# Attention block on one core: keys laid on the partitions for the scores, where queries lay before

## The chip, the cores and the metric

The kernel runs on one core of a Trainium2 chip. Its engines each run their own stream of instructions and meet through semaphores: TensorE (PE, matmuls and weight loads), VectorE (DVE), ScalarE (ACT), GpSimd (POOL) and SyncE (SP, which here issues DMAs). The metric is device time in microseconds (us) of one launch; lower is better.

## What is computed

The reference, cut to what matters (bfloat16 inputs; B = 8 batches of 112 queries, 32 heads of 192, 512 cached keys, model width 640):

```python
q = (x @ wq).reshape(8, 112, 32, 192).transpose(0, 2, 1, 3)
scores = einsum("bhqd,bhkd->bhqk", q, k_cache) * 192 ** -0.5
p = softmax(scores)                          # over the 512 keys
o = einsum("bhqk,bhkd->bhqd", p, v_cache)
out = o.transpose(0, 2, 1, 3).reshape(8, 112, 32 * 192) @ wo
```

The caches hold 50 MB each, wq and wo 7.9 MB each.

## The kernel before

`build_mha_kernel` works on pairs of heads: 4 groups of 8 heads, in each group 8 batches, in each batch 4 pairs, 128 pairs in all. Every engine's program is a loop over pairs (`run_program`), in which each stage has a fixed place and a lag: `DEFAULT_ORDERS` lists for each engine which stage of which pair is issued in one period. The order is written out by hand, and each stage begins with waits on semaphores (`W`).

For one pair the stages are:

- **Q** (`pe_Q`, L262): 15 matmuls of 112 columns give q transposed (head dimension on the partitions) for two heads; ACT copies it out (L272) and DVE makes four half copies (L323 to L326), so that each head of 192 stands as one chunk of 128 and one half-filled chunk.
- **S** (`pe_S`, L166 to L169): 8 matmuls of 256 columns with q as weights and K as moving operand. Scores come with the 112 queries on the partitions and 512 keys along the row. K has been transposed on its way in by the DMA (`issue_k`, L477).
- **Softmax**: DVE finds each row's maximum while it copies the scores (L332), ACT takes the exponential and the row sum (L284), DVE the reciprocal (L344) and, per head, a diagonal matrix of reciprocals (L308).
- **PT** (`pe_PT`, L182): 8 matmuls with the probabilities as weights and the diagonal as moving operand transpose and normalise at once; ACT (L278) and DVE (L338) copy the result out.
- **PV** (`pe_PV`, L200 and L206): 16 matmuls of 112 columns with V as weights; L206 uses 64 columns of the array for each of two heads. ACT copies the output out (L291).
- **O** (`pe_O`, L234 and L235): 6 matmuls of 512 and 128 columns with wo, accumulated over the 4 pairs of a batch; after the last of them DVE adds the sum to `acc` in float32 (L373 to L377, `dve_oacc`), and in the last group writes the output tile.

K and V come in blocks of 4 heads (768 KB each) on SP's queue, into six buffers each; a block is issued when the block that used its buffer has been consumed. The weights come on POOL's queue, paced by waits on the K and V blocks. x is transposed by TensorE at the start (L402, L409).

Of the kernel before, what the change touches and what calls it, by code (L numbers as in the profile page):

```python
# [5 lines left out]

BF16 = mybir.dt.bfloat16
F32 = mybir.dt.float32
ACTF = mybir.ActivationFunctionType
ALU = mybir.AluOpType  # L10

DEFAULT_ORDERS = dict(
    PE=[("S", 0), ("PT0", -1), ("PV", -2), ("PT1", -1), ("O", -3), ("Q", 2)],
# [7 lines left out]
def build_mha_kernel(nc, x, k_cache, v_cache, wq, wo, out, cfg=None):  # L21
    cfg = dict(cfg or {})
    B, SQ, D = x.shape
    _, H, SK, DH = k_cache.shape
# [3 lines left out]
    DC = D // 128  # L28
# [8 lines left out]
    scale = float(DH) ** -0.5  # L37
# [31 lines left out]

    with ExitStack() as es:  # L70
        def sb(name, shape, dt):
            return es.enter_context(nc.sbuf_tensor(name, shape, dt))

        def sem(name):
            return es.enter_context(nc.semaphore(name))

        WQC = HG * DH
        wq_sb = sb("wq_sb", [128, 2, DC, WQC], BF16)
        wo_sb = sb("wo_sb", [128, 2, 3 * PPU, D], BF16)
        OUTT = cfg.get("OUTT", False)  # L80
        if OUTT:
            accT = sb("accT", [128, B, DC, SQ], F32)
            oTf = sb("oTf", [128, 2, DC, SQ], BF16)
            acc = None
        else:
            acc = sb("acc", [SQ, B, D], F32)
        xT_sb = sb("xT_sb", [128, DC, B * SQ], BF16)
        kt = [sb(f"kt{j}", [128, 2, 3, G * 128], BF16) for j in range(NKB)]
        vt = [sb(f"vt{j}", [128, G, 768], BF16) for j in range(NVB)]
        qs = sb("qs", [128, NQ, NSLOT, SQ], BF16)  # L90
        s_sb = sb("s_sb", [SQ, NSS, SK], F32)
        p_sb = sb("p_sb", [SQ, NP, SK], BF16)
# [4 lines left out]
        ident = sb("ident", [128, 128], BF16)  # L97
        nmx = sb("nmx", [SQ, NS], F32)
        rsum = sb("rsum", [SQ, NS], F32)
        rinv = sb("rinv", [SQ, NS], F32)  # L100
        ps = es.enter_context(nc.psum_tensor("ps", [128, 8, 512], F32))

        sS = sem("sS"); sPT = sem("sPT"); sPV = sem("sPV"); sO = sem("sO"); sQ = sem("sQ")
        dSM = sem("dSM"); dDG = sem("dDG"); dQC = sem("dQC"); dPTE = sem("dPTE"); dOA = sem("dOA"); dRC = sem("dRC")
        aEX = sem("aEX"); aQE = sem("aQE"); aPTE = sem("aPTE"); aPVE = sem("aPVE")
        gI0 = sem("gI0"); gINIT = sem("gINIT"); dINIT = sem("dINIT")
        sOF = sem("sOF"); aOF = sem("aOF")
        mX = sem("mX")
# [4 lines left out]
        mK = [sem(f"mK{j}") for j in range(NKB)]  # L113
        mV = [sem(f"mV{j}") for j in range(NVB)]
        mOUT = [sem(f"mOUT{j}") for j in range(2)]
# [3 lines left out]
        mWQ = [sem(f"mWQ{j}") for j in range(min(2, NHG) * PPU)]  # L119
        mWO = [sem(f"mWO{j}") for j in range(min(2, NHG) * PPU)]  # L120
# [23 lines left out]
        block = es.enter_context(nc.Block())  # L144

        def W(eng, s, v):
            if v > 0:
                eng.wait_ge(s, v)
# [120 lines left out]
        def act_evacQ(act, ip):  # L269
            W(act, sQ, ip + 1)  # L270
            W(act, sS, 2 * (ip - NQ) + 2)
            act.activation(qs[:, ip % NQ, 0:3, :], ps[:, 5, 0:3 * SQ].rearrange("p (c s) -> p c s", c=3),  # L272
                           ACTF.Copy).then_inc(aQE, 1)

        def act_evacpT0(act, ip):
            W(act, sPT, 2 * ip + 1)
            W(act, sPV, ip - NPT + 1)
            act.activation(pT_sb[:, ip % NPT, 0, :], ps[:, 2, 0:4 * SQ], ACTF.Copy).then_inc(aPTE, 1)  # L278

        def act_exp(act, i, h):  # L280
            Hh = 2 * i + h
            W(act, dSM, Hh + 1)
            W(act, sPT, Hh - NP + 1)
            act.activation(p_sb[:, Hh % NP, :], s_sb[:, Hh % NSS, :], ACTF.Exp,  # L284
                           bias=nmx[:, Hh % NS:Hh % NS + 1], scale=-1.0,
                           accum_out=rsum[:, Hh % NS:Hh % NS + 1]).then_inc(aEX, 1)

        def act_evacPV(act, ip):
            W(act, sPV, ip + 1)
            W(act, sO, ip - NO + 1)  # L290
            act.activation(oT_sb[:, ip % NO, :, :], ps[:, 4, 0:3 * SQ].rearrange("p (c s) -> p c s", c=3),  # L291
                           ACTF.Copy).then_inc(aPVE, 1)

        def act_evacOF(act, ip):
# [3 lines left out]
            W(act, sOF, b + 1)  # L298
            act.activation(o_out[:, b, :], psb[0:SQ, 7, 256:256 + D], ACTF.Copy).then_inc(aOF, 1)

# [3 lines left out]
        def dve_diag(dve, ip, h):  # L304
# [3 lines left out]
            dve.tensor_scalar(dg[:, Hh % ND, :], ident[0:SQ, 0:SQ], rinv[:, Hh % NS:Hh % NS + 1], None,  # L308
                              op0=ALU.mult).then_inc(dDG, 1)

# [17 lines left out]
        def dve_smax(dve, i, h):  # L328
            Hh = 2 * i + h
            W(dve, sS, Hh + 1)  # L330
            W(dve, aEX, Hh - NSS + 1)
            dve.tensor_scalar(s_sb[:, Hh % NSS, :], ps[0:SQ, h, :], -scale, None, op0=ALU.mult,  # L332
                              op1=ALU.min, accum_out=nmx[:, Hh % NS:Hh % NS + 1]).then_inc(dSM, 1)

# [11 lines left out]
        def dve_oacc(dve, ip):  # L346
# [6 lines left out]
            if OUTT:  # L353
# [3 lines left out]
                for k, (src, cs) in enumerate(parts):  # L357
# [6 lines left out]
                    else:  # L364
                        ins = dve.tensor_tensor(dst, src, accT[:, b, cs, :], op=ALU.add)
                ins.then_inc(dOA, 1)
                return
            parts = [(ps[0:SQ, 6, :], slice(0, 512)), (ps[0:SQ, 7, 0:128], slice(512, 640))]
            for k, (src, cs) in enumerate(parts):
# [4 lines left out]
                elif hg < NHG - 1:  # L374
                    ins = dve.tensor_tensor(acc[:, b, cs], src, acc[:, b, cs], op=ALU.add)
                else:
                    ins = dve.tensor_tensor(o_out[:, b, cs], src, acc[:, b, cs], op=ALU.add)  # L377
            ins.then_inc(dOA, 1)
# [5 lines left out]
        psb = ps[:].bitcast(BF16)  # L384
# [27 lines left out]
        def run_program(eng, stages, order, hook=None, post_hook=None):  # L412
            for i in PER:
                if hook is not None:
                    hook(eng, i)
                for st, lag in order:
                    ip = i + lag
                    if ok(ip):
                        stages[st](eng, ip)
                if post_hook is not None:  # L420
                    post_hook(eng, i)
# [24 lines left out]
        def _(act):  # L446
            W(act, dINIT, 1)
            act.activation(dummy[:, 2:3], dummy[:, 0:1], ACTF.Exp)
            run_program(act, ACT_STAGES, orders["ACT"])
# [211 lines left out]
    return nc  # L661


def bass_standalone__mha_block_cached__near_ridge_kernel(
    nc: bass.Bass,
    x: bass.AP,
    k_cache: bass.AP,
    v_cache: bass.AP,
    wq: bass.AP,
    wo: bass.AP,  # L670
    out: bass.AP,
):
    return build_mha_kernel(nc, x, k_cache, v_cache, wq, wo, out)


# [26 lines left out]
```

## Time and profile before

| What | Value |
|---|---|
| median of 3 runs | 500.41 us (499.59 to 500.98) |
| span of the profiled execution, first to last instruction | 499.2 us |
| TensorE busy, share of the span | 96% |
| VectorE, ScalarE, GpSimd | 89%, 71%, 14% |
| bytes moved by DMA, mean rate | 119.90 MB, 240 GB/s |
| mean granted TensorE clock | 0.999 |

The page of the profile counts each engine's busy time, cuts the span in 40 slices, follows the chain of work that ended last back from the last instruction, and groups instructions by line, engine and shape, with the mean duration of one and the idle time before it. The timeline lists instructions in order of time and merges neighbours of one line ("x8"). Matmuls are pipelined: one starts while the one before it is still passing through the array, so the cost of a matmul in a dense stretch is the distance between two starts, not its duration.

### The profile page before, as it was taken

The page shows a single profiled execution, that of the slowest core. Times are in us where ns is not written, and L with a number is a line of the kernel's source. Part 1 is how long each engine was busy: PE and PEld are TensorE (multiplying, and loading weights), DVE is VectorE, ACT ScalarE, POOL GpSimd, SP SyncE. Part 2 cuts the span into 40 slices and gives each one's busy share as a digit, 9 for nine tenths or more (in the row PEclk, how much of TensorE's full clock was granted, in tenths as well). Part 3 has the DMA queues.
Part 4 walks back from the last instruction along what each step waited for, and adds up shares of the span by engine and source line. Part 5 has one row for each costly group of instructions (what it writes and reads, how often), then busy time and mean ns, then how long its engine had stood idle before and what let it go on. Part 6 is the DMA issues. An engine that isn't in the chain of part 4 may idle for free.

```text
span 499.2 us, 18678 instructions
## 1 busy us (share of the span) xinstructions
PE 479.0 (96%) x6824; PEld 418.9 (84%) x6824; DVE 446.6 (89%) x1610; ACT 355.1 (71%) x898; POOL 71.5 (14%) x133
## 2 busy tenths in 40 slices
PE   1799999999999999999999999999999999999995
PEld 1788888888888888888888888888888888888884
DVE  2589999998999999999999999999999999999994
ACT  1277777777777777777777777777777777777773
POOL 7110133131000133131000122322000000000000
PEclk9999999999999999999999999999999999999999
DMA  9999999999999999999999999999999999999000
GB/s 227 305 285 239 244 256 274 249 265 292 237 249 263 281 261 259 245 265 251 239 247 236 259 290 279 240 282 260 233 272 254 255 260 255 238 258 261 3 14 25
DMA packets 239738, 119.90 MB, mean 240 GB/s; under 512 B 201840, under 2 KB 236480, under 8 KB 239648
## 3 DMA queue, kind: packets, MB, share of 16 engines
q1 hardware_dynamic: 233472, 101.82, 94.4%
q0 software_dynamic: 6176, 16.88, 11.3%
q8 instruction: 56, 0.92, 0.8%
q14 instruction: 34, 0.28, 0.2%
HBM read 67.21 MB, written 1.15 MB: 137 GB/s over the span
## 4 chain that ended last, share of the span: by engine, by line
PE 93%; DMA 2%; issue 1%; DVE 1%; POOL 1%; ACT 0%; DVEq 0%; POOLq 0%; ACTq 0%
PE ps L262 19%; PE ps L234 16%; PE ps L182 13%; PE ps L200 10%; PE ps L206 8%; PE ps L166 6%; PE ps L169 6%; PE ps L167 6%; PE ps L168 6%; PE ps L235 4%; DMA wq_sb<-in_wq_dram 2%; DVE xT_sb L409 1%; POOL wq_sb L578 0%; DVE s_sb L332 0%; DVE o_out L377 0%
## 5 line engine op out<-in xcount | busy, mean ns | idle before, releaser
L284 ACT ACTIVATE p_sb<-s_sb,nmx 112x512 bf16<-112x512 f32 x256 | 181.6, 712 | 3.1 <-DVE s_sb L332 2.1
L332 DVE TENSOR_SCALAR_CACHE_REDUCE s_sb<-ps 112x512 f32<-112x512 f32 x256 | 166.3, 686 | 16.2 <-PE ps L169 14.0
L278 ACT ACTIVATE pT_sb<-ps 128x448 bf16<-128x448 f32 x128 | 69.5, 543 | 88.4 <-PE ps L182 88.4
L262 PE MATMUL ps<-xT_sb,wq_sb 128*128 128x112 bf16 x1920 | 118.0, 215 | 5.2 <-DMA wq_sb<-in_wq_dram 5.2
L234 PE MATMUL ps<-wo_sb,oT_sb 128*112 128x512 bf16 x384 | 118.3, 380 | 0.0
L262 PEld LDWEIGHTS ps<-xT_sb,wq_sb 128*128 128x128 bf16 x1920 | 103.8, 99 | 16.7 <-DMA wq_sb<-in_wq_dram 4.4
L182 PE MATMUL ps<-dg,p_sb 112*128 112x112 bf16 x1024 | 94.0, 214 | 1.8 <-ACT p_sb L284 1.6
L272 ACT ACTIVATE qs<-ps 128x336 bf16<-128x336 f32 x128 | 57.6, 450 | 45.0 <-PE ps L262 41.8
L338 DVE CAST pT_sb<-ps 128x448 bf16<-128x448 f32 x128 | 79.9, 624 | 5.3 <-PE ps L182 1.4
L235 PE MATMUL ps<-wo_sb,oT_sb 128*112 128x128 bf16 x384 | 83.9, 219 | 0.0
L182 PEld LDWEIGHTS ps<-dg,p_sb 112*128 112x128 bf16 x1024 | 64.5, 98 | 14.4 <-ACT p_sb L284 1.9
L166 PE MATMUL ps<-kt,qs 128*112 128x256 bf16 x256 | 70.8, 277 | 2.5 <-issue 1.9
L200 PE MATMUL ps<-pT_sb,vt 128*128 128x112 bf16 x1024 | 71.8, 213 | 0.1
L167 PE MATMUL ps<-kt,qs 128*112 128x256 bf16 x256 | 70.4, 275 | 0.0
L169 PE MATMUL ps<-kt,qs 128*112 128x256 bf16 x256 | 70.4, 275 | 0.0
L168 PE MATMUL ps<-kt,qs 128*112 128x256 bf16 x256 | 70.3, 275 | 0.0
L234 PEld LDWEIGHTS ps<-wo_sb,oT_sb 128*112 128x112 bf16 x384 | 49.7, 129 | 22.3
L581 POOL DMA_DIRECT2D wq_sb<-in_wq_dram x60 | 32.1, 539 | 188.5 <-DMA kt<-in_k_cache_dram 182.4
L308 DVE TENSOR_SCALAR dg<-ident,rinv 112x112 bf16<-112x112 bf16 x256 | 52.9, 249 | 5.0 <-issue 0.5
L200 PEld LDWEIGHTS ps<-pT_sb,vt 128*128 128x128 bf16 x1024 | 56.5, 98 | 0.9 <-issue 0.5
L291 ACT ACTIVATE oT_sb<-ps 128x336 bf16<-128x336 f32 x128 | 55.3, 432 | 1.7 <-PE ps L206 1.7
L235 PEld LDWEIGHTS ps<-wo_sb,oT_sb 128*112 128x112 bf16 x384 | 50.0, 130 | 0.0
(38 smaller groups left out, 498.5 us busy)
## 6 DMA issues: line engine op xcount, KB each, us to landing
vt<-in_v_cache_dram SPq DMA_DIRECT2D x64, 768.0 KB, 5.8
wq_sb<-in_wq_dram POOLq DMA_DIRECT2D x60, 96.0 KB, 5.3
wo_sb<-in_wo_dram POOLq DMA_DIRECT2D x24, 160.0 KB, 5.6
wo_sb<-in_wo_dram POOLq DMA_DIRECT2D x32, 80.0 KB, 5.1
wq_sb<-in_wq_dram POOLq DMA_DIRECT2D x4, 480.0 KB, 10.2
wo_sb<-in_wo_dram POOLq DMA_DIRECT2D x4, 320.0 KB, 10.9
out_dram<-o_out SPq DMA_DIRECT2D x8, 140.0 KB, 4.4
kt<-in_k_cache_dram SPq DMA_TRANSPOSE x64, 9.9
```

Source lines behind the costliest of these rows:

```text
L166: pe.matmul(bk[:, 0:256], qs[:, qb, EA[h], :], ktb[:, :, 0, cs], start=True, stop=False)
L167: pe.matmul(bk[:, 0:256], qs[:, qb, ET[h], :], ktb[:, :, 1, cs], start=False, stop=True)
L168: pe.matmul(bk[:, 256:512], qs[:, qb, OC[h], :], ktb[:, :, 2, cs], start=True, stop=False)
L169: pe.matmul(bk[:, 256:512], qs[:, qb, OH[h], :], ktb[:, :, 1, cs], start=False, stop=True).then_inc(sS, 1)
L182: mm = pe.matmul(ps[:, 2 + h, j * SQ:(j + 1) * SQ], p_sb[:, pslot, j * 128:(j + 1) * 128], dg[:, dslot, :], start=True, stop=True)
L200: pe.matmul(ps[:, 4, oc * SQ:(oc + 1) * SQ], vtb[:, u, q * 192: q * 192 + 128], pT_sb[:, ptb, h, j * SQ:(j + 1) * SQ], start=(j == 0), sto ...
L234: pe.matmul(ps[0:SQ, 6, :], oT_sb[:, ob, c, :], wo_sb[:, wb, 3 * lp + c, 0:512], start=first, stop=last)
L235: mm = pe.matmul(ps[0:SQ, 7, 0:128], oT_sb[:, ob, c, :], wo_sb[:, wb, 3 * lp + c, 512:640], start=first, stop=last)
L262: mm = pe.matmul(ps[:, 5, c * SQ:(c + 1) * SQ], lhsT, xT_sb[:, dc, b * SQ:(b + 1) * SQ], start=(dc == 0), stop=(dc == DC - 1))
L284: act.activation(p_sb[:, Hh % NP, :], s_sb[:, Hh % NSS, :], ACTF.Exp, bias=nmx[:, Hh % NS:Hh % NS + 1], scale=-1.0, accum_out=rsum[:, Hh % ...
L332: dve.tensor_scalar(s_sb[:, Hh % NSS, :], ps[0:SQ, h, :], -scale, None, op0=ALU.mult, op1=ALU.min, accum_out=nmx[:, Hh % NS:Hh % NS + 1]). ...
L338: dve.tensor_copy(pT_sb[:, ip % NPT, 1, :], ps[:, 3, 0:4 * SQ]).then_inc(dPTE, 1)
```

## The change

A new function `build_main` computes the whole block; the old `build_mha_kernel` stays behind it as a second path. It runs only if a flag says that some sum of exponentials fell out of the range 2^-30 to 2^40.

```diff
-    return build_mha_kernel(nc, x, k_cache, v_cache, wq, wo, out)
+    with nc.sbuf_tensor("flag", [1, 1], I32) as flag:
+        build_main(nc, x, k_cache, v_cache, wq, wo, out, flag)
+        raised = nc.values_load(flag[0:1, 0:1], ...)
+        with nc.If(raised != 0):
+            build_mha_kernel(nc, x, k_cache, v_cache, wq, wo, out)
```

`build_main` works in 64 units: 8 groups of 4 heads, in each 8 batches. Head `a` of a unit has the band of partitions 32a to 32a+31.

- **K** comes in whole rows, 16 consecutive keys of a head in one partition (6144 bytes); DVE transposes blocks of 32 x 32 words (a word is a pair of bfloat16) in four instructions per unit. The four instructions take the keys 4 apart, and write words 4 apart:

```diff
+            def do_KT(u, t):
+                src = kr[u % NK][:, t:16:4, :].bitcast(I32).rearrange("p s (c i) -> p c s i", c=3)
+                dst = kt[u % 2][:, t].rearrange("p c j e -> p c (j e)").bitcast(I32).rearrange("p c (j s) -> p c s j", s=4)
+                dve.transpose(dst, src).then_inc(vKT, 1)
```

- **S**: keys are the weights, q moves; the score tile has 128 keys on the partitions and 112 queries along the row. Each matmul contracts over one band of 32 partitions; six of them per tile make up 192.

```diff
+                W(pe, vKT, 4 * (u + 1))
+                W(pe, aEX, 4 * u)
+                for t in range(4):
+                    for c in range(6):
+                        for a in range(4):
+                            p = slice(32 * a, 32 * a + 32)
+                            mm = pe.matmul(ps[:, a, SQ * t:SQ * (t + 1)], kt[u % 2][p, t, c // 2, :, c % 2],
+                                           qT[g % 2][p, c, SQ * b:SQ * (b + 1)], start=(c == 0), stop=(c == 5))
```

- **Softmax**: ACT takes the exponential straight from PSUM, 4 instructions of 128 x 448 per unit, with no maximum subtracted, into `pT`, whose 112 queries are padded to 128 columns.
- **PV**: the probabilities are the weights, V moves, with a column of ones beside it, so that each matmul of 193 columns gives the output and the row sum. V comes in two halves (768 bytes per piece), each with its own column of ones.

```diff
+                        o0, v0 = (0, 31) if t % 2 == 0 else (1, 32 + DH)
+                        mm = pe.matmul(pv[:, k, e, o0:o0 + DH + 1], pT[u % 2][:, a, t, :],
+                                       vs[u % NV][:, a, t // 2, v0:v0 + DH + 1], start=(t == 0), stop=(t == 3), ...)
```

- **NM** (DVE): add the two sums, take the reciprocal, clear one column of PSUM, multiply the four heads' outputs by their reciprocals. POOL counts reciprocals that are out of range.
- **T**: 6 transposes by TensorE put the output's head dimension on the partitions; ACT copies the 672 columns out (`tevac`).
- **Q** and **O** are cut into items: Q in 96 items (5 matmuls of 448 columns, copied by ACT), O in 112 (6 matmuls of 320 columns, added to `acc` by DVE). They take turns in two PSUM banks, and each waits until its bank has been read. wq's columns are put in the order of the bands by POOL (`reorder`, for the groups after the first; the first group uses four column quarters of the array instead).

The order on TensorE, and on DVE, for unit u:

```diff
+            for u in range(NU + 1):
+                if u < NU:
+                    do_S(u)
+                if u > 0:
+                    do_PV(u - 1)
+                for it in items_at[u][0]:
+                    do(it)
+                if u > 0:
+                    do_T(u - 1)
+                for it in items_at[u][1]:
+                    do(it)
...
+                for t in kts[:2]:
+                    do_KT(u + 1, t)
+                if u > 0:
+                    do_NM(u - 1)
+                for t in kts[2:3]:
+                    do_KT(u + 1, t)
+                for it in oe[0]:
+                    do_OE(it)
+                for t in kts[3:]:
+                    do_KT(u + 1, t)
+                for it in oe[1]:
+                    do_OE(it)
```

Six units in eight have one Q and two O (the first Q and the first O before T, the other O behind it), one has two Q and two O, one has four Q.

All loads are on SP's queue: x, the first blocks of wq and wo, then K and V of each unit in turn (three K buffers, four V buffers), with the later weight blocks between them. `load_k(u)` waits until unit u-3 has been transposed, `load_v(u)` until PV(u-4) is done.

More of the change, by code (lines that the diff above doesn't have):

```diff
@@ L8 @@
 F32 = mybir.dt.float32
+I32 = mybir.dt.int32
 ACTF = mybir.ActivationFunctionType
@@ L71, in sb @@
         def sb(name, shape, dt):
-            return es.enter_context(nc.sbuf_tensor(name, shape, dt))
+            return es.enter_context(nc.sbuf_tensor("g_" + name, shape, dt))
         def sem(name):
-            return es.enter_context(nc.semaphore(name))
+            return es.enter_context(nc.semaphore("g_" + name))
         WQC = HG * DH
@@ L100, in build_mha_kernel @@
         rinv = sb("rinv", [SQ, NS], F32)
-        ps = es.enter_context(nc.psum_tensor("ps", [128, 8, 512], F32))
+        ps = es.enter_context(nc.psum_tensor("g_ps", [128, 8, 512], F32))
         sS = sem("sS"); sPT = sem("sPT"); sPV = sem("sPV"); sO = sem("sO"); sQ = sem("sQ")
@@ L672, in bass_standalone__mha_block_cached__near_ridge_kernel @@
 ):
-    return build_mha_kernel(nc, x, k_cache, v_cache, wq, wo, out)
+    with nc.sbuf_tensor("flag", [1, 1], I32) as flag:
+        build_main(nc, x, k_cache, v_cache, wq, wo, out, flag)
+        raised = nc.values_load(flag[0:1, 0:1], min_val=0, max_val=1 << 20,
+                                skip_runtime_bounds_check_because="a count of sums out of range")
+        with nc.If(raised != 0):
+            build_mha_kernel(nc, x, k_cache, v_cache, wq, wo, out)
+    return nc
 _INS = ['x', 'k_cache', 'v_cache', 'wq', 'wo']
```

348 lines of the change are left out of this document (added).

## The prediction

> **What bounds the kernel now.** I read the page first, then the chain of waits in order of time, then one pair of heads in the timeline.
>
> ```profile
> span 499.2 us, 18678 instructions
> PE 479.0 (96%) x6824; PEld 418.9 (84%) x6824; DVE 446.6 (89%) x1610; ACT 355.1 (71%) x898; POOL 71.5 (14%) x133
> ...
> PEclk9999999999999999999999999999999999999999
> ...
> q1 hardware_dynamic: 233472, 101.82, 94.4%
> ...
> PE 93%; DMA 2%; issue 1%; DVE 1%; POOL 1%; ACT 0%; DVEq 0%; POOLq 0%; ACTq 0%
> ```
>
> The chain that ends last is TensorE for 93% of the span, at full clock. DVE at 89% and the DMA queue at 94.4% stand just behind. The chain shows the period of one pair:
>
> ```profile
> 248.59 0.74 PE ps L262 x15
> 252.24 0.74 PE ps L262 x15
> ```
>
> 252.24 - 248.59 = 3.65 us, and 128 pairs make 467 us; some 32 us of start, waits and end complete the span. Inside a pair (columns: start, duration, group):
>
> ```profile
> 250.04 0.36 PE L182 MATMUL ps<-dg,p_sb 112*128 112x112 bf16 x4
> 250.24 0.56 PE L200 MATMUL ps<-pT_sb,vt 128*128 128x112 bf16 x8
> 250.73 0.39 PE L206 MATMUL ps<-pT_sb,vt 128*64 128x112 bf16 x8
> 251.05 0.37 PE L182 MATMUL ps<-dg,p_sb 112*128 112x112 bf16 x4
> 251.26 0.38 PE L234 MATMUL ps<-wo_sb,oT_sb 128*112 128x512 bf16 x1
> 251.48 0.22 PE L235 MATMUL ps<-wo_sb,oT_sb 128*112 128x128 bf16 x1
> 251.53 0.38 PE L234 MATMUL ps<-wo_sb,oT_sb 128*112 128x512 bf16 x1
> ...
> 252.07 0.90 PE L262 MATMUL ps<-xT_sb,wq_sb 128*128 128x112 bf16 x15
> 252.81 0.28 PE L166 MATMUL ps<-kt,qs 128*112 128x256 bf16 x1
> 252.92 0.27 PE L167 MATMUL ps<-kt,qs 128*112 128x256 bf16 x1
> ```
>
> From start to start, 15 matmuls of 112 columns take 0.74 us (0.049 each), one of 256 takes 0.11, and 512 plus 128 take 0.27 (251.26 to 251.53). All fit 0.0025 + columns x 0.000417 us. TensorE streams columns without a gap, so only fewer columns make it faster. Two exceptions matter. The 8 of L200 take 0.49 where 8 x 0.049 is 0.39, and L206 to L182 loses as much: a change between whole and half arrays costs about 0.10 us. And L206's two halves start together; cut to 254.375 to 254.385, the timeline answers
>
> ```profile
> 254.38 0.24 PE L206 MATMUL ps<-pT_sb,vt 128*64 128x112 bf16 x2
> ```
>
> so both starts lie within 0.01 us, and 8 such matmuls pay for 4.
>
> **The change, TensorE.** The work goes from 128 pairs to 64 units of four heads. Per unit:
> - S: 96 matmuls of 112 columns, each on a band of 32 partitions, four bands to four PSUM banks. No row shows row bands. Bounds: 0.049 per four, if they start together as L206's halves do; 4 x 0.049 = 0.197, if they follow one another as L182's do. I take 0.049, L206 being the only row with a divided array: 24 x 0.049 + two changes at 0.10 = 1.38.
> - PV: 16 of 193 columns at 0.083 = 1.33. The 8 transposing matmuls per pair (L182) are gone with the diagonals.
> - T: 6 of 112 columns = 0.30.
> - Q: 96 items over 64 units, each 5 of 448 columns = 0.946. The 12 items of the first group use four column quarters; as with L206 they cost the same, else up to four times (34 us more at the start).
> - O: 112 items, each 6 of 320 columns = 0.815.
>
> Sum: 1.38 + 1.33 + 0.30 + 1.5 x 0.946 + 1.75 x 0.815 = 5.85 us a unit, 375 us for 64, against 467.
>
> **DVE, and the wait that takes its place.**
>
> ```profile
> L332 DVE TENSOR_SCALAR_CACHE_REDUCE s_sb<-ps 112x512 f32<-112x512 f32 x256 | 166.3, 686 | 16.2 <-PE ps L169 14.0
> L375 DVE TENSOR_TENSOR acc<-ps,acc 112x512 f32<-112x512 f32 x16 | 10.9, 682 | 0.0
> L375 DVE TENSOR_TENSOR acc<-ps,acc 112x128 f32<-112x128 f32 x16 | 4.5, 280 | 0.0
> L344 DVE RECIPROCAL rinv<-rsum 112x2 f32<-112x2 f32 x128 | 21.2, 166 | 4.5 <-ACT p_sb L284 0.6
> L278 ACT ACTIVATE pT_sb<-ps 128x448 bf16<-128x448 f32 x128 | 69.5, 543 | 88.4 <-PE ps L182 88.4
> L272 ACT ACTIVATE qs<-ps 128x336 bf16<-128x336 f32 x128 | 57.6, 450 | 45.0 <-PE ps L262 41.8
> ```
>
> Row maxima, diagonals, half copies of q and L338's cast leave DVE. From L375's two forms, 384 elements more cost 0.402 us, so a DVE instruction pays 0.146 + elements x 0.00105. New per unit: four transposes of 384 words, for which no row exists. Bounds: 0.55 (one pass) and 0.95 (every word costs two). I take 0.55, since the rows here go at one element per step. NM is a reduce (0.15), a reciprocal (0.17, L344), a memset (0.15), a product of 768 (0.95) and their hand-overs: 1.55 in all. Each O evacuation of 320 is 0.48.
>
> [...]
>
> The hand-overs count:
>
> ```profile
> 250.44 0.54 ACT L278 ACTIVATE pT_sb<-ps 128x448 bf16<-128x448 f32 x1 [0.62 <-PE ps L182]
> ```
>
> L182's four end their streams at 250.24 and ACT starts at 250.44: 0.20 from TensorE to its reader. Back I take 0.10 (an estimate: in
>
> ```profile
> 490.68 0.41 DVE L308 TENSOR_SCALAR dg<-ident,rinv 112x112 bf16<-112x112 bf16 x2
> 491.00 0.10 PEld L182 LDWEIGHTS ps<-dg,p_sb 112*128 112x128 bf16 x1 [1.88 <-ACT p_sb L284]
> ```
>
> the first of two diagonals ends near 490.9).
>
> Now the common iteration, six in eight, with one Q and two O: S(u) and PV(u-1) until 2.71; then q0 to 3.66, o0 to 4.47; T waits for NM; then o1. TensorE alone needs 1.38 + 1.33 + 0.95 + 1.63 + 0.30 = 5.58. DVE starts NM at 2.91 and ends at 4.46, ready for T. But in DVE's order a third transpose, then o0's evacuation, then the fourth transpose stand behind NM, and S(u+1) waits for the fourth: 4.46 + 0.55 + 0.48 + 0.55 + 0.10 = 6.13. So DVE's queue holds TensorE back by 0.55. What waits behind S(u+1) is everything on TensorE. The iteration with two Q and two O (u mod 8 = 4) is TensorE's own 6.52, that with four Q (u mod 8 = 2) 6.77. Mean: (6 x 6.13 + 6.52 + 6.77) / 8 = 6.26 us.
>
> Hidden beside this: ACT's four exps, 1.5 Q copies and one copy of 672 elements, by L278 and the step to L272 (0.00083 per element): 4 x 0.55 + 1.5 x 0.54 + 0.73 = 3.74 of 6.26. The exps end 3.8 us into the iteration, before o1 needs q0's bank. POOL's reorders and range counts are read one group and four units later.
>
> **DMA.** The transposing loads go; K comes in rows of 6144 B, V in pieces of 768 B: 1.57 MB a unit, 1.82 with weights. In the window 453 to 463, in quarter microseconds, the last V load runs alone in the middle:
>
> ```profile
> GB/s 230 103 84 290 291 288 293 288 293 289 291 305 125 49 68 43 61 221 362 381 387 307 332 362 454 349 367 379 374 369 379 353 138 61 26 26 15 0 0 33
> ```
>
> That is about 365 GB/s with pieces of 1536 B: 5.0 us a unit, hidden under 6.26. SP's loads wait for KT(u-3) and PV(u-4), so they run about three iterations ahead. The cover fails below 1.82 / 6.26 = 291 GB/s.
>
> **Start and end.**
>
> ```profile
> 0.00:25.00 25.00, 12.06 (x101) 10.93 (x102) 9.61 (x26) 4.46 (x9) 11.73 (x22) 1.00 0.99 266
> ```
>
> ```profile
> 7.15 0.62 PE L402 MATMUL ps<-ident,vt 112*128 112x112 bf16 x5 [7.15 <-DMA vt<-in_x_dram]
> ...
> 495.88 0.89 DVE L377 TENSOR_TENSOR o_out<-ps,acc 112x512 bf16<-112x512 f32 x2 [2.78 <-PE ps L235]
> ```
>
> One SP queue brings x, two blocks of wq, one of wo and K and V in turn; K3 is behind 9.6 MB. At 0.30 MB per us, between the 266 GB/s of the first 25 us and the 365 above, that is 32 us; with about 3 to land and 2.2 for its transposes S(3) starts at 37 (bounds 30 and 43). 61 iterations follow, then PV 1.33, two O 1.63, T 0.30, its copy 1.03, two O 1.63 and an evacuation 0.68: 6.6. The store takes what it takes now, from 495.88 + 0.89 to the span's end, 2.4. Then every engine loads the flag and jumps over the old kernel; no row shows either, bounds 0 and 10 (the nearest stretch of that kind is this kernel's start, 7.15 to its first matmul); I take 6. End: 15.
>
> **Sum.** 37 + 61 x 6.26 + 15 = 434 us of span; the median of the runs, 500.4, lies 1.2 above the profiled span, so **435 us**.
>
> **Rivals.**
> 1. *The strided transposes are slow* (0.95). The chain behind NM becomes 6.94 in the seven iterations with O; mean 6.92, 37 + 422 + 16 = 475 us. For it: the words step by 16 bytes, which no access of the old kernel does. Against it: nothing here shows such a price.
> 2. *The row bands don't run together* (slower than before). Place: the 96 matmuls of S. Each 0.01 us per four adds 0.24 an iteration, 15.4 in all; 65 us are to spare, so it decides from 0.049 + 0.042 = 0.091 us per four, about twice my value. At 0.197 (one after another) the result is 435 + 15.4 x 14.8 = 663. At half overlap, 0.10, it is 514. Against it: the L206 row of two. For it: that row shows halves by columns and two at once, not bands by rows and four. [...]
> 3. *DMA binds.* The page's mean over the old span is 240 GB/s; at that rate 1.82 MB take 7.58 a unit and the time is 37 + 462 + 16 = 515. For it: V's pieces are half as long. Against it: the old mean is with transposing loads, which the window shows at about 290 while they run; without them 365. At 280 GB/s it is 6.5 a unit, 450.
> 4. *The change doesn't do what it says*: a sum out of range sends the kernel through the old path too, about 435 + 500. The scores are small by the reference's scaling, so I leave it at 0.01.
>
> **Chances.** Forecast (transposes near one pass, bands together) 0.50, within 404 to 447: below, by TensorE's own 5.85 an iteration and a start of 31; above, by 6 us more at start and end together with 0.1 in each hand-over chain. Slow transposes 0.28, 447 to 482. DMA 0.07, 450 to 515. Bands apart 0.13, 485 to 663, almost all of it above 500. Old path and others 0.02. For 8 in 10 the range is 404 to 482: it holds the first two cases and part of the third. A difference under 0.3% can't be told from none. Faster 0.85, same 0.01, slower 0.14.
>
> **What would show it.** S as 24 starts of fours about 0.05 apart, 1.4 us a unit; transposes of 0.55 us; S(u+1) released by DVE's fourth transpose, TensorE idle about 0.5 us there in six of eight iterations; units 6.1 to 6.8 us apart; DMA below full. I am wrong if the fours spread to 0.1, if transposes take 0.9, if TensorE waits for K or V loads, or if the start or the jump at the end takes over 10 us more than allowed.

## The result, and the profile after

The changed kernel takes 465.57 us (median of 4 runs, 462.46 to 467.97), the kernel before 500.00 (median of 4, 498.68 to 500.98): a ratio of 0.929, 95% interval 0.924 to 0.935. The forecast was 435, in a range of 404 to 482. So the direction is right and the gain is half of what was forecast: 34 us instead of 65. (Medians are of all runs; the ratios, here and below, use only runs within 1.5% of the fastest of the same kernel, so the two can differ a little.)

The page of the changed kernel, its profiled execution with a span of 465.0 us (busy time and share of each engine; DMA queues with packets, MB and share; the chain that ended last; groups of instructions with busy time, mean ns of one, and idle time before them):

```profile
span 465.0 us, 20206 instructions
PE 397.8 (86%) x8920; PEld 295.3 (64%) x8920; DVE 320.4 (69%) x634; ACT 220.0 (47%) x421; POOL 76.3 (16%) x280
...
q1 hardware_dynamic: 90256, 118.70, 77.8%
q8 instruction: 72, 1.18, 1.0%
...
PE 58%; DVE 23%; issue 14%; DMA 2%; ACT 1%; SPq 0%; POOL 0%; DVEq 0%; POOLq 0%
...
L940 DVE STREAM_TRANSPOSE kt<-kr 128x384 int32<-128x384 int32 x256 | 206.4, 860 | 8.3 <-DMA kr<-in_k_cache_dram 8.3
```

TensorE is busy 86% where it was 96%, DVE 69% where it was 89%, and the DMA queue 78% where it was 94%. Nothing is full. The chain has two parts that stood at 1% before: DVE with 23% and "issue" with 14%. That 14% is not yet the missing time: two of the runs below, which have hardly any of the pauses that this section comes to, still show 12% there. A transpose costs 860 ns, not 550.

The timeline of TensorE over one common iteration (columns: start, duration, group, idle time before):

```profile
250.69 1.36 PE L836 MATMUL ps<-qT,kt 32*128 32x112 bf16 x96 [0.52 <-DVE kt L940]
251.98 1.52 PE L850 MATMUL ps<-vs,pT 128*128 128x193 bf16 x16
253.34 1.11 PE L801 MATMUL ps<-xT,wqs 128*128 128x448 bf16 x5
254.28 0.98 PE L817 MATMUL ps<-wos,oT 128*128 128x320 bf16 x6
255.10 0.46 PE L859 MATMUL ps<-ident,os 112*128 112x112 bf16 x6
255.40 0.98 PE L817 MATMUL ps<-wos,oT 128*128 128x320 bf16 x6
256.90 1.30 PE L836 MATMUL ps<-qT,kt 32*128 32x112 bf16 x72 [0.53 <-DVE kt L940]
```

From S to S are 6.21 us (forecast 6.13). S's 96 matmuls take 1.29 (250.69 to 251.98; forecast 1.38), and S(u+1) waits 0.53 us for DVE's transposes (forecast 0.55). DVE's side of the same iteration, in its own timeline:

```profile
253.54 0.17 DVE L945 TENSOR_REDUCE sm<-ps 112x4 f32<-112x8 f32 x1 [1.09 <-PE ps L850]
253.74 0.18 DVE L948 RECIPROCAL rinv<-sm 112x4 f32<-112x4 f32 x1
253.92 0.06 DVE L949 MEMSET ps<- 128x4 f32 x1
254.02 0.96 DVE L952 TENSOR_TENSOR os<-ps,rinv 112x768 bf16<-112x768 f32 x1
254.90 0.86 DVE L940 STREAM_TRANSPOSE kt<-kr 128x384 int32<-128x384 int32 x1
255.61 0.47 DVE L966 TENSOR_TENSOR acc<-ps,acc 128x320 f32<-128x320 f32 x1
256.00 0.84 DVE L940 STREAM_TRANSPOSE kt<-kr 128x384 int32<-128x384 int32 x1
```

The order is the one that was forecast: NM, a transpose, the evacuation of o0 (the first O item), the fourth transpose, and 0.06 later S. So the common iteration doesn't hold the missing 30 us. They lie in a few places like these, TensorE's timeline around 215 us:

```profile
213.04 1.36 PE L836 MATMUL ps<-qT,kt 32*128 32x112 bf16 x96 [0.53 <-DVE kt L940]
214.34 0.60 PE L850 MATMUL ps<-vs,pT 128*128 128x193 bf16 x5
218.85 1.37 PE L850 MATMUL ps<-vs,pT 128*128 128x193 bf16 x10 [3.92 <-issue]
```

TensorE stops for 3.92 us in the middle of PV, between two matmuls with no semaphore between them (one of PV's 16 is missing from the trace). The waits (us in total, times, longest) show where that happens:

```profile
PE ps L850 <- issue: 11.3, 6, 3.9
...
PE ps L836 <- issue: 6.7, 5, 3.4
...
PE ps L801 <- issue: 4.2, 3, 2.6
```

Ten such pauses, each of 1.0 to 3.9 us, lie near 25, 37, 45, 52, 118, 124, 136, 215, 297 and 304 us. What was late is seen in the DMA view, first of the 7.4 us up to 216.4, then of the 1.2 us behind them:

```profile
DMA packets 1837, 1.95 MB, mean 263 GB/s; under 512 B 59, under 2 KB 1796, under 8 KB 1837
...
q1 hardware_dynamic: 1837, 1.95, 81.3%
```

```profile
q1 hardware_dynamic: 106, 0.47, 98.5%
q8 instruction: 1, 0.02, 5.1%
```

The queue q8, named "instruction", moved 72 packets of 16 KB (1.18 MB) over the span, one in 6.5 us on average. That it brings the program itself is read from its name, and from the half-score run below, where 6144 fewer instructions came with 24 fewer packets. In the 7.4 us to 216.4 there is none; then one comes while the data queue takes 98.5% of the engines. It has landed by 217.4, and TensorE goes on 1.45 later. The trace's packets show the same at all ten pauses: each ends 1.2 to 1.6 us after an instruction packet has landed. They show, too, how soon TensorE runs out: the pauses at 52, 215 and 304 us begin 6.9, 7.1 and 7.1 us after the packet before had landed. That fits some 1.4 us to its first use and then one packet's worth of instructions (an estimate: the 256 of the half-score run, out of the 270 that the common iteration has in 6.21 us, are 5.9). Four of the five longest cost more than their length. The windows behind this one show it (columns: window, length, busy time and count of PE, PEld, DVE, ACT and POOL, then granted clock, DMA share and GB/s):

```profile
217.00:219.00 2.00, 0.15 (x2) 0.15 (x3) 0.00 (x0) 0.00 (x0) 0.00 (x0) 1.00 0.62 250
219.00:221.00 2.00, 2.00 (x14) 1.50 (x13) 0.51 (x4) 0.00 (x0) 0.11 (x1) 0.59 0.07 26
221.00:223.00 2.00, 2.00 (x9) 0.98 (x8) 1.64 (x2) 0.54 (x1) 1.49 (x5) 0.56 0.68 168
223.00:225.00 2.00, 2.00 (x19) 1.42 (x18) 1.58 (x4) 0.73 (x1) 0.00 (x0) 1.00 0.74 236
```

After the pause TensorE runs some 4 us at 0.59 and 0.56 of its clock: about 1.7 us more (0.41 and 0.44 of 2 us each).

### The profile page after: what moved, and what is told of

It reads as the page before. It is cut to its first block, busy times and chain, and to the rows that moved or that the text cites. A ratio compares the mean times of both kernels' runs of the same rounds, so it can differ in the third digit from the quotient of the medians.

```text
span 465.0 us, 20206 instructions
## 1 busy us (share of the span) xinstructions
PE 397.8 (86%) x8920; PEld 295.3 (64%) x8920; DVE 320.4 (69%) x634; ACT 220.0 (47%) x421; POOL 76.3 (16%) x280
## 3 DMA queue, kind: packets, MB, share of 16 engines
q1 hardware_dynamic: 90256, 118.70, 77.8%
q8 instruction: 72, 1.18, 1.0%
## 4 chain that ended last, share of the span: by engine, by line
PE 58%; DVE 23%; issue 14%; DMA 2%; ACT 1%; SPq 0%; POOL 0%; DVEq 0%; POOLq 0%
PE ps L850 21%; PE ps L836 19%; DVE kt L940 12%; PE ps L801 10%; PE ps L817 5%; DVE acc L966 3%; PE ps L806 3%; DVE os L952 2%; DVE rinv L948 2%; DVE sm L945 2%; DMA xs<-in_x_dram 2%; PE ps L859 1%; ACT pT L901 1%; DVE ps L949 0%; DVE acc L963 0%
## 5 line engine op out<-in xcount | busy, mean ns | idle before, releaser
L940 DVE STREAM_TRANSPOSE kt<-kr 128x384 int32<-128x384 int32 x256 | 206.4, 860 | 8.3 <-DMA kr<-in_k_cache_dram 8.3
L901 ACT ACTIVATE pT<-ps 128x448 bf16<-128x448 f32 x256 | 118.6, 549 | 109.9 <-PE ps L836 109.9
L836 PE MATMUL ps<-qT,kt 32*128 32x112 bf16 x6144 | 88.2, 208 | 30.2 <-DVE kt L940 23.5
L850 PE MATMUL ps<-vs,pT 128*128 128x193 bf16 x1024 | 101.3, 252 | 11.6 <-issue 11.3
L817 PE MATMUL ps<-wos,oT 128*128 128x320 bf16 x672 | 109.9, 300 | 1.2 <-ACT oT L910 0.8
L836 PEld LDWEIGHTS ps<-qT,kt 32*128 32x128 bf16 x6144 | 77.3, 93 | 52.5 <-DVE kt L940 43.3
L801 PE MATMUL ps<-xT,wqs 128*128 128x448 bf16 x420 | 93.7, 359 | 4.2 <-issue 4.2
L850 PEld LDWEIGHTS ps<-vs,pT 128*128 128x128 bf16 x1024 | 85.0, 99 | 18.9 <-issue 12.9
L817 PEld LDWEIGHTS ps<-wos,oT 128*128 128x128 bf16 x672 | 62.9, 98 | 28.5 <-issue 1.4
L952 DVE TENSOR_TENSOR os<-ps,rinv 112x768 bf16<-112x768 f32 x64 | 61.3, 958 | 2.2
```

What stands on the lines that cost most here:

```text
L801: mm = pe.matmul(ps[:, bank(it), 0:HQ], wqs[:, g % 2, dc, 128 * c:128 * (c + 1)], rhs, start=(dc == 0), stop=(dc == DC - 1))
L817: mm = pe.matmul(ps[:, bank(it), 0:HO], oT[:, c, 128 * m:128 * (m + 1)], wos[:, g % 2, c, HO * h:HO * (h + 1)], start=(c == 0), stop=(c == 5))
L836: mm = pe.matmul(ps[:, a, SQ * t:SQ * (t + 1)], kt[u % 2][p, t, c // 2, :, c % 2], qT[g % 2][p, c, SQ * b:SQ * (b + 1)], start=(c == 0), s ...
L850: mm = pe.matmul(pv[:, k, e, o0:o0 + DH + 1], pT[u % 2][:, a, t, :], vs[u % NV][:, a, t // 2, v0:v0 + DH + 1], start=(t == 0), stop=(t == ...
L901: act.activation(pT[u % 2][:, a, :, 0:SQ], ps[:, a, 0:4 * SQ].rearrange("p (t q) -> p t q", t=4), ACTF.Exp, scale=scale).then_inc(aEX, 1)
L940: dve.transpose(dst, src).then_inc(vKT, 1)
```

## The experiments

The theory: TensorE outruns the delivery of its own instructions whenever the loads hold a packet up. The rivals: the slow transposes and DVE's order are what costs (so the common iteration must be shortened), or the bytes themselves.

**The transposes' step alone.** The changed kernel with one edit; the columns of K come out in another order, so the keys meet other keys' values.

```diff
-                dst = kt[u % 2][:, t].rearrange("p c j e -> p c (j e)").bitcast(I32).rearrange("p c (j s) -> p c s j", s=4)
+                dst = kt[u % 2][:, t].rearrange("p c j e -> p c (j e)").bitcast(I32).rearrange("p c (s j) -> p c s j", s=4)
```

> DVE's transposes write neighbouring words in place of every fourth (the keys then stand in another order than V's rows, so the products pair other keys and values; the work is the same). If the step of 16 bytes is what makes them 0.86 us, they fall to about 0.55, the common iteration from 6.21 to TensorE's own 5.6 or 5.7, and the time from 465 to about 440. Rival: a transpose of 384 words costs 0.86 whatever the step; then nothing changes, 465.

Measured: 448.58 and 465.23 us in two runs (no interval), not the 440 expected. From the groups of the page of the first:

```profile
L940 DVE STREAM_TRANSPOSE kt<-kr 128x384 int32<-128x384 int32 x256 | 135.5, 555 | 11.1 <-DMA kr<-in_k_cache_dram 11.1
```

The same transpose takes 555 ns when it writes neighbouring words and 860 when it writes every fourth: the step alone costs 0.305 us. The common iteration falls from 6.21 to 5.69 us, since S waits for DVE hardly at all. But 0.52 us in some 45 iterations would be 23 us, and the first run is only 17 us below the changed kernel, the second level with it. Two runs so far apart can't say how much of the time the step is worth. TensorE's waits on "issue" stay: 26 us in all in the first run, against 24 in the changed kernel.

**The loads alone.** K and V are loaded only into their buffers' first round (three units of K, four of V); every later unit computes on those.

```diff
-                    W(sp, vKT, 4 * (u - NK + 1))
+                    return
...
-                    W(sp, pPV, u - NV + 1)
+                    return
```

> Leaves out all K and V loads but the first three and four (later units use old data); the instructions on TensorE, DVE and ACT stay the same. Theory: the gaps on TensorE that the profile puts down to issue are waits for its own instructions, whose 16 KB pages queue behind the loads on the DMA engines. Then the gaps of 1 to 4 us vanish (those of the start, which has the weight loads, in part) and the time is 435 to 442. Rival: the pages come too slowly for this many small instructions whatever else runs; then the gaps stay and the time is 460 or more.

Measured: 440.52 us, ratio 0.879 (0.875 to 0.883), 25 us less than the changed kernel. Its page and its waits:

```profile
q1 hardware_dynamic: 18112, 23.53, 16.3%
q8 instruction: 71, 1.16, 1.1%
```

```profile
PE ps L836 <- DVE kt L940: 26.0, 48, 1.0
...
PE ps L836 <- issue: 3.2, 3, 2.1
```

As many instruction packets come, and the common iteration is the same 6.21 with the same wait for DVE. Only the pauses are gone, all but two at the start, where the few loads are in flight: "issue" falls from 24 to 5 us, and none of the changed kernel's four stretches at half clock behind a pause (1.7 us each) is left. That is 19 and 7 us, about the 25. So the loads make the pauses, and the pauses make the difference. This run alone can't say whether TensorE's demand for instructions has a part in it.

**The demand alone.** All loads stay; half of each score's contraction is left out (three chunks of six), so 96 fewer of TensorE's instructions per unit.

```diff
-                    for c in range(6):
+                    for c in range(3):
```

> The changed kernel with only the first three of six contraction steps in S (left out: half of each score), so that TensorE has 96 instructions fewer a unit; all loads and all DVE and ACT work stay. S falls from 1.3 to 0.7 us, the common iteration from 6.21 to 5.6. If the gaps come from the number of instructions against the loads, the sum of gaps over 0.75 us behind the first S falls from about 24 us to under 8 and the time is 405 to 418. Rival: the pages wait behind the loads however few they are; then the gaps stay above 18 us and the time is 425 to 435.

Measured: 400.83 us, ratio 0.802 (0.800 to 0.803), below even what was expected. Its page, its waits and TensorE's timeline:

```profile
q1 hardware_dynamic: 90256, 118.70, 89.4%
q8 instruction: 48, 0.79, 0.8%
```

```profile
PE ps L836 <- DVE kt L940: 25.4, 47, 1.0
...
PE ps L836 <- issue: 0.7, 1, 0.7
```

```profile
254.74 0.77 PE L836 MATMUL ps<-qT,kt 32*128 32x112 bf16 x48 [0.52 <-DVE kt L940]
...
260.35 0.77 PE L836 MATMUL ps<-qT,kt 32*128 32x112 bf16 x48 [0.51 <-DVE kt L940]
```

The matmuls that were left out save 0.60 us an iteration (6.21 to 5.61), 38.4 us over 64 units; the time falls by 64.7. The other 26 are the pauses, gone although the same bytes now come faster: the queue is at 89.4% instead of 77.8%. So it isn't the bytes either, but instructions against bytes. 6144 fewer instructions (3072 matmuls and their weight loads) take 24 fewer packets: one packet feeds 256 instructions, 128 matmuls. The kernel before bears this out: there a packet came every 8.9 us, here every 8.3, both beside fuller data queues than the changed kernel's (94.4% and 89.4% against 77.8%), and TensorE's waits on "issue" were 1.9 us there and 0.7 here.

**DVE's order alone.** Three transposes go ahead of NM, the fourth right behind it, and both O evacuations come last, so that S isn't held.

```diff
-                for t in kts[:2]:
+                for t in kts[:3]:
...
-                for t in kts[2:3]:
-                    do_KT(u + 1, t)
-                for it in oe[0]:
-                    do_OE(it)
...
-                for it in oe[1]:
+                for it in oe[0] + oe[1]:
```

> DVE's order changed: the third transpose stands before NM, the fourth right behind NM and before both O evacuations; nothing else. If the fourth transpose behind o0's evacuation holds back S(u+1), the wait of S for DVE vanishes, the common iteration falls from 6.21 to 5.6 or 5.7 and the time to about 442. Rival: what is gained on DVE is given back as more waiting for instructions and loads, since TensorE then needs 1.82 MB per 5.8 us; then 455 or more. Second rival: T waits for a later NM; then 465.

Measured: 466.22 us, ratio 0.928 (0.922 to 0.933): no gain. The timeline and the waits of TensorE:

```profile
251.03 1.36 PE L836 MATMUL ps<-qT,kt 32*128 32x112 bf16 x96
...
256.64 0.67 PE L836 MATMUL ps<-qT,kt 32*128 32x112 bf16 x40
...
257.73 0.48 PE L836 MATMUL ps<-qT,kt 32*128 32x112 bf16 x24 [0.41 <-issue]
```

```profile
PE ps L850 <- issue: 17.7, 7, 4.1
PE ps L836 <- issue: 17.6, 15, 3.9
```

The iteration is 5.61 instead of 6.21 and S no longer waits for DVE. What was won there goes into waits on "issue", 47 us in all instead of 24. This profile is of the longest of the four runs, 474.23, so its 47 may be too large for the others; the same edit on the kernel with small weights, further down, shows the same in two profiles of equal length. The wait for DVE had been covering for late instructions.

**Smaller blocks of weights.** The later weight blocks of 960 KB come in pieces of 160 to 192 KB, one or two a unit, and the result is whole.

```diff
-                if b == 3 and g + 2 < NG:
-                    load_wq(g + 2)
-                if b == 6 and g + 1 < NG:
-                    load_wo(g + 1)
+                if b >= 3 and g + 2 < NG:
...
+                    sp.dma_start(wqr[:, dc], wq[128 * dc:128 * (dc + 1), 4 * DH * g2:4 * DH * (g2 + 1)]).then_inc(mWP[dc], 16)
+                if b in (6, 7) and g + 1 < NG or b < 4 and g > 0:
...
+                    sp.dma_start(wos[:, g1 % 2, c], wo[4 * DH * g1 + 128 * c:4 * DH * g1 + 128 * (c + 1)]).then_inc(mWO[g1 % 2], 16)
```

> The later blocks of wq and wo (960 KB each) come in pieces of 192 and 160 KB, one per unit, in place of one load each. If the gaps at 118 to 138, 215 and 304 us come from a weight block standing in the same stretch as a K and a V load, they vanish or shrink, and the time falls by 8 to 15 us to 450 to 457; the gaps of the start stay. Rival: the pages wait behind K and V alone; then no change, 465.

Measured: 459.48 us, ratio 0.919 (0.914 to 0.925), 6 us less, short of the 450 to 457 expected. Waits on "issue" fall from 24 to 17 us, the pause of 3.92 becomes two of 1.73 and 2.18. So the weight blocks look like a part of it, not all. It has the lowest median of the kernels here whose result is whole, but its interval still touches that of the changed kernel (0.925 against 0.924), so the gain is not quite clear of the spread.

**Order and small weights together**, the last two diffs in one kernel.

> DVE's new order together with the small weight pieces. If the order's gain was eaten by waits for instructions that stand behind whole weight blocks, both together give 445 to 452. Rival: at 5.62 us an iteration the loads leave too little room for the pages anyway; then 458 or more, no better than the small pieces alone.

Measured: 460.92 us, ratio 0.922 (0.914 to 0.930): no better than small weights alone. The two profiled spans are alike (455.2 and 455.4), with the common iteration at 5.62 instead of 6.21 and 34 us of waits on "issue" instead of 17: what DVE gave, the waits for instructions took.

**Dense writes with the right keys.** With the small weights and the dense write, K's rows are loaded so that the dense order is the right one: four loads of 32 partitions each, in runs of 1536 B.

```diff
+                for a in (0, 2, 1, 3):
+                    sp.dma_start(kr[u % NK][32 * a:32 * a + 32].rearrange("p (s t) d -> p s (t d)", t=4),
+                                 k_cache[b, 4 * g + a].rearrange("(s j t) d -> j s (t d)", s=4, t=4)).then_inc(mK[u % NK], 16)
```

> Dense transposes with the keys in V's order, on top of the small weight pieces: K comes in four loads of 32 partitions, each partition in four runs of four keys (1536 bytes), so that neighbouring words are the right keys; same bytes. Theory (the step of four words makes the transposes slow, the rest is waiting for instructions behind loads): transposes 0.55 us, common iteration 5.7, time 438 to 448. Rival: loads of 32 partitions or of shorter runs move slower than one of 128 (K lands later than the 5.8 us of the changed kernel), DVE waits for K and TensorE's instruction pages wait longer; then 460 or more.

Measured: 519.46 us, ratio 1.037 (1.034 to 1.041): slower than the old kernel. Its page and its waits:

```profile
q1 hardware_dynamic: 118848, 118.72, 95.8%
```

```profile
DVE kt L941 <- DMA kr<-in_k_cache_dram: 74.3, 25, 14.4
...
PE ps L837 <- issue: 29.6, 20, 3.6
```

The same bytes fill the queue to 95.8% of a longer span, DVE waits for K, and the pauses grow to 61 us. The four-word step is the price for K's whole rows, and here it is the lower price.

**Loads held back.** If a deep queue of loads delayed the packets, a shallow one should help. On the kernel with small weights, from unit 6 on, the first half of V waits until the V before it has landed, the second until its own K has:

```diff
+                    if u >= 6:
+                        W(sp, *((mV[(u - 1) % NV], 32 * ((u - 1) // NV + 1)) if h == 0 else (mK[u % NK], 16 * (u // NK + 1))))
                     sp.dma_start(vs[u % NV][:, :, h, 32:32 + 2 * DH],
```

> The kernel with the small weight blocks, and SP holds the V halves back from unit 6 on: the first half of V waits until both halves of the unit before have landed, the second until its own K has landed, so that no more than about 1.3 MB is queued at a time. Theory (instruction pages wait behind a backlog of loads): the pauses inside TensorE's sequences after 60 us shrink from about 13 us to under 5, median 450 to 455. Rival (the pages are delayed by the loads' mere rate, and holding loads back only makes them later): pauses stay, DVE or TensorE begins to wait for K or V, 458 to 475.

> As the paced kernel, and DVE takes three transposes ahead of NM, the fourth right behind it, and both O evacuations last. Theory (backlog is the cause): with pages in time the shorter common iteration of 5.62 us shows, 430 to 445. Rival (a shorter iteration needs pages and loads faster than both can come at once): no better than the paced kernel, 453 to 475.

Measured: 491.68 us (ratio 0.978, 0.971 to 0.984), and with DVE's new order 496.23 (median of eight runs from 485.63 to 507.16; ratio 0.981, 0.976 to 0.986), both slower than either range expected. The waits of the first, in the longest of its four runs (504.33):

```profile
DVE kt L941 <- DMA kr<-in_k_cache_dram: 99.7, 43, 7.4
...
PE ps L837 <- issue: 4.8, 4, 1.7
```

The rival has the right mechanism, at a higher price than it named: the loads come too late (43 waits for K), and "issue" still takes 16 us where small weights alone leave 17. So the depth of the queue isn't shown to be what delays the packets; how exactly the loads do it stays open.

## Why the prediction was right in direction and half wrong in size

**What held.** *The row bands run together.* S took 1.29 us for 24 fours, 0.054 each with the change back to the whole array in it; the second rival fell. *DVE's fourth transpose holds S*: 0.53 us in the common iteration, 23.5 us in 45 waits over the span. The iterations with two Q and two O, and with four Q, are 6.56 and 6.83 (forecast 6.52 and 6.77). *DMA doesn't bind*: after the start, DVE and TensorE wait for no load (the last such wait, 8.3 us of DVE for the first K, ends at 26.67 us).

**Sizes that were off and cancelled.** From NM's start to S(u+1) the forecast has 1.55 + 0.55 + 0.48 + 0.55 + 0.10 = 3.23; the timeline of DVE has 1.36 + 0.71 + 0.39 + 0.84 + 0.06 = 3.36. The first rival's mechanism is real: the step of four words costs 860 ns against 555 in the first experiment. But it didn't cost the 475 of that rival: neighbours on DVE overlap (a transpose is followed after 0.71, not 0.86, the evacuation after 0.39, not 0.47), NM was shorter by 0.19 and the hand-over by 0.04. That the forecast of 6.13 came so near 6.21 is in part luck: the two transposes in this chain were 0.45 dearer than forecast, the other three terms 0.32 cheaper. (The prediction's own terms give 6.14, 6.53 and 6.79 where it has 6.13, 6.52 and 6.77, less than 1 us in the sum.)

**The sum.** Of the 31 us by which the span of 465.0 misses 434, 6 lie ahead of S(3) (42.9 instead of 37, with 4.7 of pauses in it), 27 in the 61 iterations (60 of them, from S(3) to S(63), average 6.72 instead of 6.26), and the end is 2 shorter (13 of the 15). Of the 27, the pauses behind S(3) take 17.5 (1.35 + 3.33 + 1.63 + 1.41 + 1.49 + 3.92 + 1.01 + 3.36) and the 0.08 of 45 common iterations 3.6. Of the rest, some 6, the granted clock explains 5.1: behind the pauses at 52, 215 and 304 us lie three stretches of 3.4 us at half clock, 1.7 each (columns as in the windows above):

```profile
55.50:58.90 3.40, 3.40 (x20) 2.57 (x19) 0.85 (x4) 0.00 (x0) 0.40 (x2) 0.50 0.16 63
219.40:222.80 3.40, 3.40 (x15) 1.94 (x13) 2.14 (x5) 0.52 (x1) 1.60 (x5) 0.50 0.37 90
308.10:311.50 3.40, 3.40 (x19) 2.38 (x17) 1.27 (x4) 0.61 (x2) 0.65 (x3) 0.50 0.15 42
```

A fourth such stretch lies ahead of S(3), behind the pause at 25. That the range holds the time is luck as well: 465 lies in the part, 447 to 482, that was meant for slow transposes, and the time came from something for which the prediction had no term and no rival.

**The step that failed** is "TensorE streams columns without a gap, so only fewer columns make it faster", carried from the old kernel to the new. There is no term for bringing TensorE its instructions. The demand could have been worked out, though not its price, for the old kernel hardly ever waits for instructions (1.9 us): the change has fewer columns in more instructions. The old kernel's page has 6824 matmuls, with as many weight loads, and

```profile
q8 instruction: 56, 0.92, 0.8%
```

one packet in 8.9 us, or 244 instructions to a packet. With the 256 of the half-score run, the forecast iteration, 135 matmuls and their weight loads in 6.13, asks for one in 5.8 (with the 244, in 5.5), and each shorter iteration for more (5.4 at 5.69 us), beside loads that here fill 77.8% of the DMA engines. The cover that the forecast named for the loads ("hidden under 6.26") held for data and failed for instructions. What they cost is known from the runs alone: ten pauses in 64 iterations, with the half clock behind four of them, some 25 us in all (26 by the half-score run, 25 by the one with few loads).

## What to carry to other kernels

Count instructions beside columns: where a change cuts wide matmuls into many narrow ones, divide the number of instructions in an iteration (matmuls and weight loads) by the 256 that went with one packet here, and ask whether so many packets can come in its time beside the loads. Here one packet every 8.9 or 8.3 us came in time beside data queues at 94.4% and 89.4%, and one every 6.5 beside 77.8% did not always. An "issue" gap in the middle of a sequence of matmuls, ending 1.2 to 1.6 us behind a packet of the instruction queue, was its mark here. As long as it stood, shortening what another engine held up brought little (DVE's new order: 466.22 us against 465.57): the wait only changed its name.

## What the runs showed of the hardware

- Four matmuls on row bands of 32 partitions, into four PSUM banks, start 0.054 us before the next four.
- A 32 x 32 transpose of 384 words per partition takes 555 ns into neighbouring words and 860 into every fourth.
- TensorE's waits on "issue" followed both the instruction packets and the loads: 72 packets with loads at 77.8% leave 24 us of waits on "issue", 71 packets with loads at 16.3% leave 5, and 48 packets with loads at 89.4% leave under 1.
- Behind four of the ten pauses (2.1, 3.3, 3.9 and 3.4 us) the granted clock was 0.50 for 3.4 us; behind one of 2.6 us it was not.
- K in four loads of 32 partitions instead of one of 128, with runs of 1536 B instead of 6144, filled the same queue to 95.8% and made the kernel slower by 60 us than the one with small weights. Partitions and run length weren't tried apart.
